# First expert of a top-2 mixture: earlier index list, transposes placed inside other products, four product banks, five output tiles

## The chip, the cores and the metric

The kernel runs on one core of one Trainium2 chip. The metric is device time in microseconds (us). Three timed runs of the kernel before gave 952.67, 953.08 and 953.52 us; the median is 953.08 us. A trace comes from one further, profiled execution that took 952.76 us.

## The reference, cut to what matters

Three stages follow one another: a linear attention with a decaying state (4 batches, 8 heads, 768 steps, head size 48), a dense block `h = ((x @ w1) * (x @ w2)) @ w3`, `y = h @ w_out`, and a mixture of 8 experts in which every row goes to its two best:

```python
logits = x @ w_gate
noisy = logits + np.log1p(np.exp(x @ w_noise)) * noise        # 3072 rows, 8 experts
top2 = np.argpartition(-noisy, 2, axis=1)[:, :2]
# softmax over the two, then per expert e, for the rows that chose it:
h = np.maximum(x[mask] @ w1[e], 0.0)                          # 384 -> 1024
out[mask] += top2_w[mask, k, None] * (h @ w2[e])              # 1024 -> 384
```

## The kernel before, in words

Rows come in 24 chunks of 128. Attention and dense block work in 12 groups of two chunks. A group `g` of the dense block has 12 steps (slots): the products of `mo_ab` with w1 (bank `bA`) and w2 (bank `bB`), and `mo_x`, which multiplies their product with the folded w3 @ w_out and accumulates in the two banks `bX`. `mo_x(g, 3)` of a group stands in the third slot of the next group; for the last group, number 11, it stands after the loop. `mo_out` then copies the gate columns into `LZ` and writes the rows to a table in HBM, `x2d` ("x_rows" in the trace). Every float32 product is made of three products of a high and a low part (`mm3`, L170 to L172), so each evicted tile is split: ScalarE writes the high part, VectorE the low one.

The gate works on batches of four chunks. `gate_top` is a generator of steps on VectorE, with two activations (exponential, logarithm with a table load before and after) on ScalarE and three small products on TensorE (L597 to L600, and L628 in the last batch). It ends with a slot number for each row and expert. `gate_put` (L638) writes row number and weight to these slots of the HBM table `slots`: one indirect DMA on GpSimd for each chunk and choice, eight a batch. The last batch but one (chunks 16 to 19) is put in slots of groups 10 and 11; the last batch (chunks 20 to 23) after group 11, beside the first expert's products.

An expert has up to 800 rows: a first half of four tiles of 128 rows, and a second of two tiles and one of 32. `need` loads the index list (`ti`, on the SyncE queue, once every put before it has landed) and gathers the rows (`xg`, indirect DMAs on GpSimd). For expert 0, `need(0, 0, ...)` takes rows of the first 20 chunks alone, so it waits for the last batch but one and not for the last; its second half takes what the last batch puts. `tr(e, hf)` transposes the gathered tiles on TensorE into banks `PB[4]` to `PB[6]` and splits them into `XTh`, `XTl`. `mm1(hf, ff)` makes one of eight blocks of the hidden layer, evicted as `HH` (high part L754 on ScalarE, low part L755 on VectorE); banks alternate between two for the first half and three for the second. `mm2(e, j)` multiplies a tile of 128 rows by w2 in eight steps of three products, scales it into an output tile `ye` (three buffers) on ScalarE, and adds it to the output with an indirect DMA on GpSimd (L780). `split_e` makes high and low parts of expert weights; `load_e` loads them.

VectorE runs in the order in which the code is written. The other engines' instructions are put in order at build time by a planner: of the instructions that its own clock says are ready, it takes the one written first. That order is then fixed; on the chip each engine goes through its list and waits where something isn't there. The functions touched by the change are `mm1`, `mm2`, the two loops over gate batches and groups, and the first expert's stretch of code after them.

Of the kernel before, what the change touches and what calls it, by code (L numbers as in the profile page):

```python
# [8 lines left out]
F32 = mybir.dt.float32  # L9
# [9 lines left out]
P = 128  # L19
B, H, S, D = 4, 8, 768, 48  # L20
DM, FF, E = 384, 1024, 8
# [3 lines left out]
NGRP = NCH // 2  # L25
# [6 lines left out]
TA, TB = 4, 2  # L32
# [39 lines left out]
def tile_kernel(ctx: ExitStack, tc: tile.TileContext, dt, nat, w3t, wout, w1, w2, e1, e2, cf, ci, out):  # L72
# [8 lines left out]
    def f(ap):  # L81
        return ap.bitcast(F32)
# [17 lines left out]
    PB = [psum.tile([P, 512], F32, name=f"pb{i}") for i in range(8)]  # L100
    bA, bB, bX, bY, bST, bK = PB[0], PB[1], (PB[2], PB[3]), PB[4], (PB[5], PB[6]), PB[7]
# [20 lines left out]
    def split(h, l, src, on=None):  # L122
        act.copy(out=h, in_=src)  # L123
        (on or dve).tensor_tensor(out=l, in0=src, in1=f(h), op=OP.subtract)  # L124
# [44 lines left out]
    def mm3(o, wh, wl, xh, xl, start, stop):  # L169
        pe.matmul(o, wh, xh, start=start, stop=False)  # L170
        pe.matmul(o, wh, xl, start=False, stop=False)  # L171
        pe.matmul(o, wl, xh, start=False, stop=stop)  # L172
# [238 lines left out]
    def at(slot, fn, *a):  # L411
        todo.setdefault(slot, []).append((fn, a))

    def run_todo(k):
        for fn, a in todo.pop(k, []):
            fn(*a)
# [101 lines left out]
    def low_p():  # L518

        while LOWP:  # L520
            l, p, h = LOWP.pop()
            dve.tensor_tensor(out=l, in0=p, in1=f(h), op=OP.subtract)

    def mo_x(g, fp):
        for tt in range(2):
            for fi in range(2):
                ff = 2 * fp + fi
                s = slice(256 * fi + P * tt, 256 * fi + P * tt + P)
                wh, wl = [w[:, ff % 4] for w in (W0, W1)[ff // 4]]
                mm3(bX[tt][:, :XW], PH[g, fp][:, s], PL[g, fp][:, s], wh, wl, ff == 0, ff == 7)  # L530

    def mo_out(g):
        for tt in range(2):
            t = 2 * g + tt
            dve.tensor_copy(out=LZ[:, t, :], in_=bX[tt][:, DM:XW])
            xo = work.tile([P, DM], F32, name="xo")
            act.copy(out=xo, in_=bX[tt][:, :DM])
            act.dma_start(out=x2d[DUMP + t * P:DUMP + P + t * P], in_=xo)
# [131 lines left out]
    EP = {}  # L670

    def open_a():
        EP["a"] = ctx.enter_context(tc.tile_pool(name="epa", bufs=1))
        XT["h"] = EP["a"].tile([P, 3, CAP], F32R, name="XTh")
        XT["l"] = EP["a"].tile([P, 3, CAP], F32R, name="XTl")
        XT["t"] = EP["a"].tile([P, DM], F32, name="xgt")
        pool.memset(XT["t"], 0.0)
        open_h(EP["a"], 0)
# [13 lines left out]
    def load_e(e, m, i):  # L692
        if m == 0 and e:
            rw = EP["b"].tile([P, 1536], F32, name="raww", bufs=2)
        else:
            rw = rawp.tile([P, 1538], F32, name="raw2", tag="raw64")[:, :1536]
        sp.dma_start(out=rw, in_=(e1, e2)[m][e, :, 1536 * i:1536 * i + 1536])
        RW[e, m, i] = rw
# [23 lines left out]
    def rows_of(j):  # L722
        return TPT if j < NT - 1 else TPL

    def ti(e, j):
        hf, jj = divmod(j, TA)
        return TI[e, hf][:rows_of(j), jj]
# [6 lines left out]
    def tr(e, hf):  # L734
        n = NAB[hf]
        for db in range(3):
            bank = PB[4 + db]
            for j in range(TA) if hf == 0 else range(TA, NT):
                o = TPT * (j - hf * TA)
                pe.transpose(bank[:, o:o + P], XG[e, j][:, P * db:P * db + P], ident)  # L740
            s = slice(hf * NAB[0], hf * NAB[0] + n)
            split(XT["h"][:, db, s], XT["l"][:, db, s], bank[:, :n])

    MB, MC, AD = (bA, bB, bK), [1], [-1]

    def mm1(hf, ff):
        n = NAB[hf]
        s0 = hf * NAB[0]
        bank = MB[ff % (2 + hf)][:, :n]
        for kb in range(3):  # L750
            w = slice(kb * FF + ff * P, kb * FF + ff * P + P)
            mm3(bank, WAh[:, w], WAl[:, w], XT["h"][:, kb, s0:s0 + n], XT["l"][:, kb, s0:s0 + n], kb == 0, kb == 2)
        n = (TA, TB)[hf] * TPT
        act.activation(out=Hh[hf][:, ff], in_=bank[:, :n], func=AF.Relu)  # L754
        dve.scalar_tensor_tensor(Hl[hf][:, ff], bank[:, :n], 0.0, f(Hh[hf][:, ff]), op0=OP.max, op1=OP.subtract)  # L755
        if hf == 1:
            dve.tensor_scalar(HM[hf][:, ff], bank[:, n:], 0.0, None, op0=OP.max)

    def mm2(e, j):
        hf, jj = divmod(j, TA)  # L760
        n, s = rows_of(j), slice(TPT * jj, TPT * jj + rows_of(j))
        MC[0] ^= 1
        bank = bX[MC[0]][:, :DM]
        y = EP["a"].tile([P, DM], F32, name="ye", bufs=3)
        wt = ti(e, j)[:, 1:2].bitcast(F32)
        if j < NT - 1:
            for ff in range(8):
                w = slice(ff * DM, ff * DM + DM)
                mm3(bank[:n], Hh[hf][:, ff, s], Hl[hf][:, ff, s], WBh[:, w], WBl[:, w], ff == 0, ff == 7)
            act.activation(out=y[:n], in_=bank[:n], func=AF.Copy, scale=wt)  # L770
        else:

            for ff in range(8):
                g = ff % 4
                pe.matmul(bank[n * g:n * g + n], HM[hf][:, ff], RW[e, 1, ff // 4][:, g * DM:g * DM + DM],  # L775
                          start=ff < 4, stop=ff > 3, tile_position=(0, n * g))
            act.activation(out=y[:n], in_=bank[:n], func=AF.Copy, scale=wt)
            for g in range(1, 4):
                dve.scalar_tensor_tensor(y[:n], bank[n * g:n * g + n], wt, y[:n], op0=OP.mult, op1=OP.add)
        ins = pool.indirect_dma_start(out=out, out_offset=bass.IndirectOffsetOnAxis(ap=ti(e, j)[:, 0:1], axis=0),  # L780
                                      in_=y[:n], in_offset=None, compute_op=OP.add).ins

        if j == 0 or AD[0] != e:
            AD[:] = [e]
        for p in AD[1:]:
            tc.declare_no_dep(ins, p, reason="an expert's rows differ")
        AD.append(ins)

    def need(e, hf, r, rows=NROW):
        load_idx(e, hf, r)  # L790
        for j in range(TA) if hf == 0 else range(TA, NT):
            gather(e, j, rows)
# [31 lines left out]
    def gate_at(o, t0, per, put):  # L824
        gen = gate_top(t0, GB)
        for i in range(10):
            at(o + i // per, next, gen, None)
        for i in range(2 * GB):
            at(o - o % SPG + put[i], gate_put, t0, i // 2, i % 2)


    for t0 in range(0, NCH - GB, GB):
        late = t0 == NCH - 2 * GB
        gate_at(SPG * ((t0 + GB) // 2) + 3, t0, 1 + late,
                (11, 11, 13, 13, 13, 14, 14, 14) if late else (13, 14, 17, 17, 19, 20, 23, 23))
    at(SPG + 2, fill_table)
    for i in range(5):
        at(2 * SPG + 6 * i, fill_out, i)
# [1 line left out]
    for g in range(NGRP):  # L840
        sub = [(mo_ab, g, 0, 0), (mo_ab, g, 0, 1), None, (mo_ab, g, 1, 0), (mo_ab, g, 1, 1), (mo_x, g, 0),
               (mo_ab, g, 2, 0), (mo_ab, g, 2, 1), (mo_x, g, 1), (mo_ab, g, 3, 0), (mo_ab, g, 3, 1), (mo_x, g, 2)]
        if g == NGRP - 1:
            attx.close()
            open_a()
            load_e(0, 0, 0)
            load_e(0, 0, 1)
        for i in range(12):
            if sub[i]:
                fn, *a = sub[i]  # L850
                fn(*a)
            elif g:
                mo_x(g - 1, 3)
                mo_out(g - 1)
            if i % 3 != 1:
                low_p()
            run_todo(SPG * g + i)
            if g == NGRP - 1:
                if i in (0, 3, 6, 9):
                    split_e(0, 0, i // 3, dve)  # L860
                    if i == 9:
                        load_e(0, 1, 0)
                        load_e(0, 1, 1)
                if i == 3:
                    need(0, 0, 0, NROW - GB * P)
    low_p()
    tr(0, 0)
    mo_x(NGRP - 1, 3)
    mo_out(NGRP - 1)
    assert not todo, todo  # L870
    t0 = NCH - GB
    gen = gate_top(t0, GB)
    for ff in range(8):
        for _ in range(2 if ff != 3 else 0):
            next(gen, None)
        mm1(0, ff)
        if ff >= 4:
            split_e(0, 1, ff - 4, dve)
    for i in range(GB):
# [5 lines left out]
    for jj in range(TA, NT):  # L885
        gather(0, jj)
    for j in range(TA):
        mm2(0, j)
        if j == 0:
            load_e(1, 0, 0)  # L890
            load_e(1, 0, 1)
            need(1, 0, 0)
    tr(0, 1)
    need(1, 1, 0)
    for ff in range(8):
        mm1(1, ff)
# [28 lines left out]
    if RMAX > 1:  # L925

        n = nc.values_load(rounds[0:1, E:E + 1], min_val=1, max_val=RMAX)
# [102 lines left out]
```

## Time and profile before

| | |
|---|---|
| timed runs, median (lowest to highest) | 953.08 us (952.67 to 953.52) |
| the profiled execution | 952.76 us, span of its trace 950.8 us |
| TensorE busy | 913.9 us, 96% of the span |
| VectorE, ScalarE, GpSimd busy | 48%, 44%, 37% |
| mean granted TensorE clock | 0.991 of full speed |

The span begins with the first instruction and ends with the last; 1.96 us lie around it. The dense block's last group ends at about 488 us, the first expert runs from there to about 552 us, and seven experts of about 55.5 us each follow. A wait names the engine and instruction that ended it.

### The profile page before, as it was taken

The numbers are of one execution on the slowest core, as the hardware profiler recorded it, in microseconds if no ns is written. First come the engines' busy times: TensorE is split into PE (matmuls) and PEld (weight loads), VectorE is DVE, ScalarE is ACT, GpSimd is POOL, SyncE is SP. The second block draws the span as 40 slices with busy tenths as digits, with TensorE's granted clock in tenths as the row PEclk, the third lists the DMA queues.
The fourth block names the chain that finished last, engine by engine and source line by source line (L and its number), as shares of the span: only waits on it lengthen the run. The fifth ranks groups of instructions, "written<-read, shape, count | busy, mean of one in ns | idle before, by whom it ended". The sixth has DMA issues, their size and how long they took to land.

```text
span 950.8 us, 17795 instructions
## 1 busy us (share of the span) xinstructions
PE 913.9 (96%) x7219; PEld 845.7 (89%) x7219; DVE 453.5 (48%) x1110; ACT 422.1 (44%) x879; POOL 347.1 (37%) x282
## 2 busy tenths in 40 slices
PE   7898999999999999999989899999999999999994
PEld 6777899999999999999979889989898998989894
DVE  5789765756756748646343263231313223131320
ACT  6767545446355445544341243433324343332420
POOL 2123100232122131140315545654557565455412
PEclk9999999999999999999999899999999999999998
DMA  9945786455242332410240464326163532614112
GB/s 359 372 148 180 192 138 205 146 155 171 79 124 79 90 112 79 132 37 18 52 150 20 86 203 149 63 66 160 39 168 62 158 62 65 161 39 103 17 20 36
DMA packets 49179, 111.64 MB, mean 117 GB/s; under 512 B 17600, under 2 KB 32192, under 8 KB 49088
## 3 DMA queue, kind: packets, MB, share of 16 engines
q1 hardware_dynamic: 33472, 85.98, 28.9%
q0 software_dynamic: 12160, 19.72, 11.5%
q10 hardware_dynamic: 3456, 4.72, 1.4%
q8 instruction: 58, 0.95, 0.5%
q14 instruction: 33, 0.27, 0.1%
HBM read 88.12 MB, written 22.27 MB: 116 GB/s over the span
## 4 chain that ended last, share of the span: by engine, by line
PE 83%; issue 4%; DVE 4%; DMA 3%; ACT 2%; POOL 2%; SPq 0%; POOLq 0%; ACTq 0%; DVEq 0%
PE pb L170 24%; PE pb L171 23%; PE pb L172 23%; PE pb L302 4%; PE pb L242 2%; PE pb L740 2%; PE pb L775 1%; PE pb L263 1%; DVE cvz L154 1%; POOL slots L643 1%; DMA slots<-g_sc,g_si 1%; DMA raw<-w 1%; PE pb L252 1%; ACT top L145 1%; DMA out<-ye,ti 1%
## 5 line engine op out<-in xcount | busy, mean ns | idle before, releaser
L170 PE MATMUL pb<-XTh,WAh 128*128 128x512 f32 (+1 forms) x384 | 134.6, 352 | 3.6 <-ACT XTh L123 3.5
L171 PE MATMUL pb<-XTl,WAh 128*128 128x512 f32 (+1 forms) x384 | 132.8, 346 | 0.0
L172 PE MATMUL pb<-XTh,WAl 128*128 128x512 f32 (+1 forms) x384 | 131.9, 346 | 0.0
L170 PE MATMUL pb<-WBh,HH 128*128 128x384 f32 x384 | 130.9, 341 | 0.7 <-ACT HH L754 0.7
L171 PE MATMUL pb<-WBl,HH 128*128 128x384 f32 x384 | 129.5, 338 | 0.0
L172 PE MATMUL pb<-WBh,HH 128*128 128x384 f32 x384 | 129.4, 337 | 0.0
L755 DVE SCALAR_TENSOR_TENSOR HH<-pb,HH 128x256 fp32r<-128x256 f32 (+1 forms) x128 | 71.4, 558 | 118.9 <-ACT HH L754 118.9
L780 POOL DMA_INDIRECT out<-ye,ti x56 | 86.8, 1550 | 112.2 <-ACT ye L770 99.0
L754 ACT ACTIVATE HH<-pb 128x256 fp32r<-128x256 f32 (+1 forms) x128 | 62.7, 491 | 130.1 <-PE pb L172 129.0
L643 POOL DMA_INDIRECT slots<-g_sc,g_si x48 | 51.5, 1073 | 119.4 <-DVE g_si L642 78.6
L770 ACT ACTIVATE ye<-pb,ti 128x384 f32<-128x384 f32 x48 | 27.9, 581 | 150.2 <-PE pb L172 102.7
L124 DVE TENSOR_TENSOR XTl<-pb,XTh 128x512 fp32r<-128x512 f32 (+1 forms) x48 | 25.3, 570 | 139.3 <-ACT XTh L123 139.2
L222 POOL TENSOR_TENSOR rku<-natc 128x384 f32<-128x384 f32 x24 | 26.9, 1119 | 174.9 <-DMA natc<-nat 103.3
L170 PE MATMUL pb<-xh,WBh 128*128 128x256 f32 x288 | 83.7, 291 | 2.9 <-DVE pp L512 2.4
L170 PEld LDWEIGHTS pb<-XTh,WAh 128*128 128x128 f32 x384 | 73.1, 191 | 14.0 <-ACT XTh L123 3.8
L170 PE MATMUL pb<-xh,WAh 128*128 128x256 f32 x288 | 82.8, 288 | 1.3 <-ACT xh L308 0.7
L172 PE MATMUL pb<-xh,WBl 128*128 128x256 f32 x288 | 81.6, 283 | 1.0 <-DVE WBl L161 1.0
L171 PE MATMUL pb<-xl,WBh 128*128 128x256 f32 x288 | 82.3, 286 | 0.0
L172 PE MATMUL pb<-xh,WAl 128*128 128x256 f32 x288 | 81.5, 283 | 0.8 <-DVE WAl L161 0.7
L171 PE MATMUL pb<-xl,WAh 128*128 128x256 f32 x288 | 81.2, 282 | 0.1
L171 PEld LDWEIGHTS pb<-XTl,WAh 128*128 128x128 f32 x384 | 73.3, 191 | 7.9
L172 PEld LDWEIGHTS pb<-XTh,WAl 128*128 128x128 f32 x384 | 72.8, 191 | 8.3
(173 smaller groups left out, 2209.0 us busy)
## 6 DMA issues: line engine op xcount, KB each, us to landing
dtc<-dt SPq DMA_DIRECT2D x24, 772.0 KB, 5.3
natc<-nat SPq DMA_DIRECT2D x24, 640.0 KB, 4.9
raw<-e SPq DMA_DIRECT2D x18, 768.0 KB, 6.3
raww<-e SPq DMA_DIRECT2D x14, 768.0 KB, 4.4
rawf<-w3t SPq DMA_DIRECT2D x16, 512.0 KB, 7.4
raw<-w SPq DMA_DIRECT2D x8, 768.0 KB, 4.4
x_rows<-xo ACTq DMA_DIRECT2D x24, 192.0 KB, 2.0
out<-zeros SPq DMA_DIRECT2D x4, 1152.0 KB, 8.1
```

The lines of the kernel that those rows point to most:

```text
L124: (on or dve).tensor_tensor(out=l, in0=src, in1=f(h), op=OP.subtract)
L170: pe.matmul(o, wh, xh, start=start, stop=False)
L171: pe.matmul(o, wh, xl, start=False, stop=False)
L172: pe.matmul(o, wl, xh, start=False, stop=stop)
L222: pool.tensor_tensor(out=t, in0=NA[j][:, :DM], in1=NA[j][:, DM:2 * DM], op=OP.mult)
L242: pe.matmul(bST[hb][:, P * a:P * a + P], KT[j][q, a].rearrange("p s i -> p (s i)"), RT[j][q, a].rearrange("p s i -> p (s i)"), start=True, ...
L302: pe.matmul(o, lt, rh, start=st, stop=en, tile_position=tp)
L643: ins = pool.indirect_dma_start(out=table, out_offset=bass.IndirectOffsetOnAxis(ap=si[:, i, k:k + 1], axis=0), in_=SC[:, i, k, :], in_offs ...
L754: act.activation(out=Hh[hf][:, ff], in_=bank[:, :n], func=AF.Relu)
L755: dve.scalar_tensor_tensor(Hl[hf][:, ff], bank[:, :n], 0.0, f(Hh[hf][:, ff]), op0=OP.max, op1=OP.subtract)
L770: act.activation(out=y[:n], in_=bank[:n], func=AF.Copy, scale=wt)
L780: ins = pool.indirect_dma_start(out=out, out_offset=bass.IndirectOffsetOnAxis(ap=ti(e, j)[:, 0:1], axis=0), in_=y[:n], in_offset=None, com ...
```

## The change

The puts of the last batch but one move from slots 11, 13 and 14 (group 10's last, and the second and third of group 11) to slots 9, 10 and 11 of group 10. `need(0, 0, ...)` moves from the fourth slot of group 11 to the second. `tr(0, 0)` moves from behind group 11 to the front of its last slot, so that two `mo_x` stand behind it and not one. The last batch's gate steps are spread otherwise over the eight `mm1(0, ff)`: before 2, 2, 2, 0, 2, 2, ... and now 5, 1, 0, 2, 1, ... These eight `mm1` go over four banks (`bA`, `bB`, `PB[4]`, `PB[5]`) in place of two. `tr(0, 1)` moves from behind `mm2(0, 3)` into its middle, before the fifth of eight steps. `ye` gets five buffers.

```diff
-    def mm1(hf, ff):
+    def mm1(hf, ff, banks=None):
         n = NAB[hf]
         s0 = hf * NAB[0]
-        bank = MB[ff % (2 + hf)][:, :n]
+        banks = banks or MB[:2 + hf]
+        bank = banks[ff % len(banks)][:, :n]
...
-    def mm2(e, j):
+    def mm2(e, j, mid=None):
...
-        y = EP["a"].tile([P, DM], F32, name="ye", bufs=3)
+        y = EP["a"].tile([P, DM], F32, name="ye", bufs=5)
...
             for ff in range(8):
+                if mid and ff == 4:
+                    mid()
...
-                (11, 11, 13, 13, 13, 14, 14, 14) if late else (13, 14, 17, 17, 19, 20, 23, 23))
+                (9, 9, 9, 10, 10, 10, 11, 11) if late else (13, 14, 17, 17, 19, 20, 23, 23))
...
         for i in range(12):
+            if g == NGRP - 1 and i == 11:
+                tr(0, 0)
...
-                if i == 3:
+                if i == 1:
                     need(0, 0, 0, NROW - GB * P)
     low_p()
-    tr(0, 0)
     mo_x(NGRP - 1, 3)
     mo_out(NGRP - 1)
...
     for ff in range(8):
-        for _ in range(2 if ff != 3 else 0):
+        for _ in range((5, 1, 0, 2, 1)[ff] if ff < 5 else 1):
             next(gen, None)
-        mm1(0, ff)
+        mm1(0, ff, (bA, bB, PB[4], PB[5]))
...
     for j in range(TA):
-        mm2(0, j)
+        mm2(0, j, (lambda: tr(0, 1)) if j == TA - 1 else None)
...
-    tr(0, 1)
     need(1, 1, 0)
```

## Rows read from the trace of the kernel before

**Rows 1.** The page, busy time of each engine: us, share, instructions.
```profile
PE 913.9 (96%) x7219; PEld 845.7 (89%) x7219; DVE 453.5 (48%) x1110; ACT 422.1 (44%) x879; POOL 347.1 (37%) x282
```

**Rows 2.** Waits of TensorE, 478 to 530 us: total us, times, longest.
```profile
PE pb L170 <- ACT XTh L123: 3.5, 1, 3.5
PE pb L740 <- DMA xg<-x_rows,ti: 2.2, 1, 2.2
PE pb L170 <- ACT HH L754: 0.7, 1, 0.7
```

**Rows 3.** TensorE by stretch: from:to, length, busy (instructions), granted clock, DMA share, GB/s.
```profile
477.88:480.06 2.18, 2.18 (x14) 1.00 0.80 207
480.06:487.84 7.78, 5.61 (x26) 0.78 0.32 133
487.84:523.30 35.46, 34.61 (x173) 1.00 0.23 69
...
527.99:540.17 12.18, 12.18 (x72) 0.76 0.62 107
540.17:544.34 4.17, 4.17 (x27) 1.00 0.00 0
544.34:545.74 1.40, 1.40 (x14) 1.00 0.00 0
551.43:552.34 0.91, 0.91 (x11) 1.00 1.04 376
552.34:569.26 16.92, 16.92 (x76) 1.00 0.63 211
569.26:578.85 9.59, 9.59 (x72) 1.00 0.01 2
```

**Rows 4.** Timeline of GpSimd: start, us, instruction, idle before it and what ended it.
```profile
452.03 0.42 POOL L677 MEMSET xgt<- 128x384 f32 x1 [25.74 <-PE pb L302]
...
467.02 1.01 POOL L643 DMA_INDIRECT slots<-g_sc,g_si  x1 [0.30 <-issue]
475.66 0.97 POOL L731 DMA_INDIRECT xg<-x_rows,ti  x1 [7.63 <-DMA ti<-slots]
...
501.76 1.01 POOL L643 DMA_INDIRECT slots<-g_sc,g_si  x1 [20.73 <-DVE g_si L623]
...
520.07 0.87 POOL L731 DMA_INDIRECT xgt<-x_rows,ti  x1 [0.30 <-issue]
```

**Rows 5.** Chain of waits, 455 to 532 us: a put from issue to landing.
```profile
467.02 5.96 DMA slots<-g_sc,g_si
...
511.39 2.74 DMA slots<-g_sc,g_si
```

**Rows 6.** Timeline of VectorE around the two gate batches and the puts.
```profile
446.46 0.22 DVE L620 TENSOR_REDUCE g_sf<-g_M 128x8 f32<-128x64 f32 x1
...
488.04 0.17 DVE L535 COPY LZ<-pb 128x16 f32<-128x16 f32 x1 [0.92 <-PE pb L172]
...
492.84 0.69 DVE L755 SCALAR_TENSOR_TENSOR HH<-pb,HH 128x512 fp32r<-128x512 f32 x1 [1.33 <-ACT HH L754]
...
496.37 0.76 DVE L584 TENSOR_TENSOR g_cm<-g_cm,g_mb 128x8 bf16<-128x8 bf16 x4
...
499.29 0.16 DVE L601 TENSOR_SCALAR g_s<-g_d 128x4 f32<-128x4 f32 x1
...
501.31 0.17 DVE L623 CAST g_si<-g_sf 128x8 int32<-128x8 f32 x1
...
505.29 0.95 DVE L710 TENSOR_TENSOR WBl<-raw,WBh 128x768 fp32r<-128x768 f32 x1
```

**Rows 7.** ScalarE ahead of the second half's splits.
```profile
527.07 0.58 ACT L770 ACTIVATE ye<-pb,ti 128x384 f32<-128x384 f32 x1 [7.19 <-DMA out<-ye,ti]
```

**Rows 8.** SyncE's queue: a weight load's issue, and waits of such loads, 440 to 545 us.
```profile
477.65 0.33 SPq L697 DMA_DIRECT2D raw<-e  x1
...
SPq L697 <- DVE WAl L710: 50.1, 2, 46.1
```

## The prediction, made before the changed kernel was run

> **What bounds the kernel now.** I read the page first: TensorE is busy 913.9 us of the 950.8 us span, the next engine 48% [rows 1]. So a change pays only where TensorE idles or runs at its lower clock, and the next view is TensorE's waits in the stretch that the change touches. There are three, 6.4 us in all [rows 2]: 2.2 us for the gathered rows in the first expert's first transposes, 0.7 us for the eviction of a bank in `mm1(0, ff)`, 3.5 us for the split of the second half's transposes. The third view, TensorE by stretch, gives each its whole price, as the granted clock shows what followed: 0.78 over the first stall and the work behind it, 0.76 over `mm1(1, ff)` behind the third, 1.00 around the second [rows 3]. [...]
>
> What each stretch would take undisturbed is read from like work:
>
> - First hole, 480.06 to 487.84: 7.78 us for twelve transposes and a `mo_x`. Undisturbed 1.40 + 2.18 = 3.58. Excess 4.20.
> - First half's products, 487.84 to 523.30: 35.46 us for eight `mm1` and four `mm2`. The next expert's eight took 16.92, a `mm2` takes 4.17, so 16.92 + 16.68 = 33.60, and about 0.05 for four tiny gate products. Excess 1.81.
> - Second hole, from 523.30 to 540.17: 16.87 us for nine transposes (0.91) and eight `mm1(1, ff)` (9.59 in the next expert). Undisturbed 10.50. Excess 6.37.
>
> All from [rows 3]; the sum, 12.38 us, is the most that the change can take away. Behind 540 us work follows without a wait of this kind and moves with it.
>
> **The change part by part, first list and first transposes.** The gate batch has its slot numbers at 446.68 us [rows 6] and GpSimd is idle for 25.74 us up to 452.03 [rows 4], so the first three puts can go out from about 447.5, while now the last starts at 467.02. Three casts then stand behind the attention's last copy at about 453; five puts at 1.27 each (0.97 busy and 0.30 of issue, [rows 4]) and the memset of 0.42 that may fall between them end by about 460. The last put starts near 458.5, 8.5 us sooner. It lands after 2.7 us or, loaded as now, 6.0 [rows 5]: 461.2 to 464.5. From landing now (472.98) to the products' restart (482.50 = 480.06 + 0.27 + 2.17) it takes 9.5 us, so the rows are there between 470.7 and 474.0. The transposes are wanted at 477.88, 2.18 us sooner than now because they stand before one more `mo_x`: 3.9 to 7.2 us to spare. The six casts and eight puts are no more than before; the SyncE queue has the list's load two slots sooner, ahead of two weight loads that wait for buffers anyway.
>
> The splits of `XTh`, `XTl` then lie beside two `mo_x` (4.36 us) in place of one. One thing is late in turn: VectorE makes three low parts of 128x512 (0.69 each for that shape, [rows 6]) before the low part that the second `mo_x` reads in its third product. Transposes done at 479.28, the last low part at about 481.1, the needed one at 481.8; wanted at 481.82. Between 0 and 0.8 us (if ScalarE takes its own product's cast first); I take 0.2. Gain 4.20 - 0.20 = **4.0 us**. `mm1(0, 0)` starts at 483.64 + 0.2.
>
> **Four banks and gate steps.** The wait of 0.7 us and what hung on it (two `mm2` steps put in its place) go, since the third block no longer needs the first's bank. The gate steps hold up the first block's low part on VectorE, but with four banks that is wanted only by the fifth block, 8.4 us after the start. The steps up to the counts end now at 497.13 [rows 6]. Shifted by 4.20, without the block that stands between them (wait 1.33 and 0.61 of its 0.69) and the next block's 0.6, they end at 490.4; three low parts of 0.6 follow, 492.2; the last steps (499.29 to 501.48, 2.19 us) end at 494.4. That is 7.1 us sooner than now. If the little exponential on ScalarE falls ahead of the second block's eviction, the low parts wait and it is 6.2; I take 6.6. The first low part is done at 491.0, wanted at 492.0: no wait.
>
> Two waits are new. The batch's count product now stands before the fourth `mm1`, which TensorE reaches at about 490.0, with the counts there at 490.4; and the batch's totals product stands in the fifth, from 492.1, and needs the slot numbers' readers, at about 493.7. All further `mm1` are queued behind both, and only TensorE waits. The planner can put them some products later, as now. Bounds 0 and 0.4, 0 and 1.6; together I take 0.8. VectorE's weight splits behind the gate end near 503.5, just as the third quarter of w2 is wanted, for nothing. Gain 1.81 - 0.80 = **1.0 us**.
>
> **Five output tiles, transposes in `mm2(0, 3)`.** Now ScalarE stands 7.19 us before the fourth `ye`, for an output add that has to land [rows 7], and the splits are queued behind it; that is the 3.5 us wait. With five buffers the fourth tile waits for nothing, and since the transposes stand before the last twelve products (2.09 us), even the splits (about 1.5 us after the transposes) are covered. What is late next is the gather. The last batch's chain is rigid from first put (501.76) to last gather (520.07) [rows 4], whose rows were there at 523.30 without a wait and, by the shortest landing of such a gather (2.3 us), not before 522.4. Shifted by 6.6 they are there between 515.8 and 516.7. TensorE wants them at 483.84 + 33.65 + 0.8 - 2.09 = 516.2. A tie: 0 to 0.5 us by these values, up to 1.6 if the gate is only 6.2 sooner and TensorE waits nowhere before. I take 0.5; a wait of 0.7 left the clock at 1.00 [rows 2, 3]. Gain 6.37 - 0.50 = **5.9 us**.
>
> [...] The eight puts take 9.63 us from the first start to the last [rows 4, 5]; seven steps at 1.01 + 0.30 make 9.2, so the VectorE work beside them, with four splits of w2 (0.95 each, [rows 6]) whose inputs both lie in SBUF, costs about 0.5 us. [...] The same splits lie beside the puts after the change.
>
> **Sum.** 4.0 + 1.0 + 5.9 = 10.9 us off the profiled execution's 952.76 (span 950.8 and 1.96 around it): 941.9. The timed runs' median is 0.32 above that execution, so I forecast 942.2 us.
>
> **Rivals.**
>
> 1. *The second half's gather is later than the tie.* The transposes stand at the head of TensorE's list with products behind them that could run. If the rows are 2 to 3 us late, TensorE waits so long and, as after the 2.2 us wait, runs on at half clock; there the excess beyond the wait was 4.20 - 2.17 = 2.0. Cost 4.0 to 5.0 in place of 0.5: gain 6.4 to 7.4, 945.7 to 946.7. For it: the chain is long, and the order is the planner's. Against it: the chain's start was worked out from measured steps. 20%.
> [...]
> 3. *The list isn't sooner.* If the last put's landing at 472.98 hangs on the transfers beside it and not on its issue, the rows come at 482.50 as now, but are wanted 2.18 us earlier: first hole 6.4 instead of none, gain 4.7, 948.4. The loaded 5.96 us against 2.74 speaks for it, the 8.5 us against it. 5%.
> 4. *Slower: the list's load is queued behind the second weight load.* These loads wait for VectorE's splits, 50.1 us for two, and the second goes out at 477.65 [rows 8]. Were the list's load behind it, the first gather would follow at about 480.3 (now 475.66) and the products restart 6.84 later, at 487.2; TensorE would idle 9.3 us from 477.88, and with 2.0 for the clock `mm1` starts 7.1 us later than now. That eats the 6.9 of the other two parts: 953.3, and by up to 3.2 us more (the loaded landing) with the weight's 768 KB in front of list and rows: 956.5. It decides from a list load after 477 us. Against it: the list's load is written before both. 6%.
>
> **How the numbers follow.** Forecast 62%, its own range 940.3 to 944.5 (nothing left of the excess, to the bounds of the new waits). Rivals 20, 3, 5 and 6%; 4% for what I don't see. The range that leaves no more than 2 in 10 out reaches over rival 1: 940.0 to 947.5. The measurement can tell about 0.2% (1.9 us) from no change: faster 0.89 (forecast, rivals 1 to 3, less 0.01), same 0.06, slower 0.05 (rival 4 and the rest, split).
>
> **What would show it.** Right: no TensorE wait on the gathered rows before 488 us; granted clock 1.00 from 477 to 545; the last put of the earlier batch near 458.5; slot numbers of the last batch near 494.9; no wait of `ye` on the output add; the next expert's first `mm1` near 541.5 in place of 552.3. Wrong: a wait on the rows of over 1 us in `mm2(0, 3)` with half clock behind it, TensorE standing before the gate's small products for over 1 us, or the list's load behind weights.

## The result, and the profile after

The changed kernel takes 943.59 us (median of five, 941.17 to 945.34), the kernel before 952.94 us beside it (five, 951.01 to 953.52). The ratio is 0.9908 [0.9889, 0.9926]. The forecast was 942.2 us, its range 940.0 to 947.5. The profiled execution took 944.56 us, its span is 942.7 us.

The page's first part: every engine's busy time is as before to 0.9 us [rows 1]. For TensorE two things cancel in it, as will be seen: less time at the lower clock behind waits, more slow products at the program's start.

```profile
PE 913.7 (97%) x7219; PEld 846.6 (90%) x7219; DVE 453.4 (48%) x1110; ACT 422.5 (45%) x879; POOL 347.7 (37%) x282
```

TensorE waits for nothing from 440 to 545 us in this trace; the three waits of [rows 2] are gone. Stretch by stretch, as in [rows 3] (from:to, length, busy time of PE, PEld, DVE, ACT and POOL, granted clock, DMA share, GB/s): the first transposes with two `mo_x`; the first half's products up to the second transposes; these with the twelve products behind them; `mm1(1, ff)`; the second half's `mm2` with the next transposes; the next expert's first eight `mm1`.

```profile
481.54:487.36 5.82, 5.82 (x38) 5.62 (x37) 3.44 (x6) 3.92 (x7) 0.00 (x0) 1.00 0.43 135
487.36:519.32 31.96, 31.92 (x162) 28.27 (x162) 15.84 (x66) 10.19 (x18) 12.38 (x13) 1.00 0.25 77
519.32:522.41 3.09, 3.09 (x22) 3.09 (x21) 1.19 (x3) 1.06 (x3) 2.48 (x3) 1.00 0.47 132
522.41:531.91 9.50, 9.50 (x73) 9.50 (x73) 3.66 (x14) 3.28 (x8) 7.67 (x7) 1.00 0.76 128
531.91:544.08 12.17, 12.17 (x88) 10.91 (x86) 5.98 (x10) 5.10 (x10) 7.46 (x6) 1.00 0.61 140
544.08:561.00 16.92, 16.92 (x76) 13.71 (x75) 9.68 (x14) 7.91 (x14) 7.20 (x6) 1.00 0.65 210
```

The clock is 1.00 in each. In the kernel before it is 0.50 from 483.00 to 485.50, behind the first wait, and 1.00 from 486.00 to 488.00; 0.50 again from 528.00 to 533.00, behind the third, and 1.00 from 534.00 to 540.00. These two values are the half and the full clock of this text; 0.78 and 0.76 [rows 3] are means over stretches that hold both. From the last `mo_ab` to `mm1(0, 0)` it takes 5.82 us (before, 477.87 to 487.84, 9.97), from there to the end of `mm1(1, ff)` 44.55 (before 52.33): 4.15 and 7.78, together 11.9 us less. The rest of the span is as long as before (410.79, before 410.63). But the span is only 8.1 us shorter, because the last `mo_ab` ends 3.67 us later, at 481.54. That comes from the very start of the program; the section on the prediction returns to it.

GpSimd, to be held against [rows 4]: first, fourth and last put of the earlier batch, its first gather, first and last put of the last batch, the first gather behind it.

```profile
451.27 1.00 POOL L643 DMA_INDIRECT slots<-g_sc,g_si  x1 [21.32 <-DVE g_si L642]
...
456.94 1.28 POOL L643 DMA_INDIRECT slots<-g_sc,g_si  x1 [0.82 <-DVE g_si L642]
...
462.90 0.97 POOL L643 DMA_INDIRECT slots<-g_sc,g_si  x1 [0.30 <-issue]
469.45 0.97 POOL L731 DMA_INDIRECT xg<-x_rows,ti  x1 [5.58 <-DMA ti<-slots]
...
498.54 1.01 POOL L643 DMA_INDIRECT slots<-g_sc,g_si  x1 [24.35 <-DVE g_si L623]
...
508.06 0.97 POOL L643 DMA_INDIRECT slots<-g_sc,g_si  x1 [0.30 <-issue]
514.07 0.98 POOL L731 DMA_INDIRECT xg<-x_rows,ti  x1 [5.04 <-DMA ti<-slots]
```

The earlier batch's first gather goes out at 469.45 in place of 475.66, in a program that is 3.67 us late: 9.9 us sooner. SyncE has the list's load (L719) ahead of the weight loads, not behind them [rows 8]:

```profile
466.46 0.33 SPq L719 DMA_DIRECT2D ti<-slots  x1
468.30 13.35 SPq L697 DMA_DIRECT2D raw<-e  x2
```

VectorE's gate [rows 6]: the last copy into `LZ` (the first product starts at 487.36), the counts, the first block's low part (now L756), the slot numbers.

```profile
487.56 0.17 DVE L535 COPY LZ<-pb 128x16 f32<-128x16 f32 x1 [0.55 <-PE pb L172]
...
493.51 0.75 DVE L584 TENSOR_TENSOR g_cm<-g_cm,g_mb 128x8 bf16<-128x8 bf16 x4
494.19 0.68 DVE L756 SCALAR_TENSOR_TENSOR HH<-pb,HH 128x512 fp32r<-128x512 f32 x1
...
498.09 0.17 DVE L623 CAST g_si<-g_sf 128x8 int32<-128x8 f32 x1
```

ScalarE around the second half's splits [rows 7]: no wait on the output add. The three casts follow one another; remember this for the last experiments.

```profile
519.84 1.06 ACT L123 CAST XTh<-pb 128x288 fp32r<-128x288 f32 x3 [1.86 <-PE pb L740]
522.61 0.58 ACT L773 ACTIVATE ye<-pb,ti 128x384 f32<-128x384 f32 x1 [1.71 <-PE pb L172]
523.80 0.39 ACT L755 ACTIVATE HH<-pb 128x256 fp32r<-128x256 f32 x1 [0.61 <-PE pb L172]
```

### The profile page after: what moved, and what is told of

It is laid out like the page before. It is cut to its first block, busy times and chain, and to the rows that moved or that the text cites. A ratio compares the mean times of both kernels' runs of the same rounds, so it can differ in the third digit from the quotient of the medians.

```text
span 942.7 us, 17789 instructions
## 1 busy us (share of the span) xinstructions
PE 913.7 (97%) x7219; PEld 846.6 (90%) x7219; DVE 453.4 (48%) x1110; ACT 422.5 (45%) x879; POOL 347.7 (37%) x282
## 4 chain that ended last, share of the span: by engine, by line
PE 90%; DVE 4%; ACT 2%; issue 2%; POOL 0%; DMA 0%; POOLq 0%; SPq 0%; DVEq 0%; ACTq 0%
PE pb L170 27%; PE pb L171 26%; PE pb L172 26%; PE pb L302 4%; PE pb L242 2%; PE pb L740 2%; PE pb L778 1%; PE pb L263 1%; DVE cvz L154 1%; PE pb L252 1%; DVE w3l L161 1%; ACT top L145 1%; PE pb L373 1%; ACT am L235 0%; DVE WBl L161 0%
## 5 line engine op out<-in xcount | busy, mean ns | idle before, releaser
L756 DVE SCALAR_TENSOR_TENSOR HH<-pb,HH 128x256 fp32r<-128x256 f32 (+1 forms) x128 | 71.3, 557 | 116.1 <-ACT HH L755 116.1
```

## The experiments

Each kernel's profile is cut in four, so that the start's share stands apart: "start" to the end of the last `mo_ab`; "hole 1" from there to `mm1(0, 0)`; "half" from there to the end of `mm1(1, ff)`; "rest". They add up to the span of that one execution. Medians are of the timed runs (their number), ratios against the kernel before run beside them. `e9` to `e12` ran on another chip than the eight ahead of them.

| kernel | median us (n) | ratio | start | hole 1 | half | rest |
|---|---|---|---|---|---|---|
| before | 952.94 (5) | | 477.87 | 9.97 | 52.33 | 410.63 |
| after | 943.59 (5) | 0.9908 [0.9889, 0.9926] | 481.54 | 5.82 | 44.55 | 410.79 |
| e1_list_back | 951.31 (10) | 0.9977 [0.9962, 0.9992] | 481.44 | 13.61 | 44.54 | 410.71 |
| e2_tr1_back | 942.14 (4) | 0.9891 [0.9870, 0.9912] | 478.47 | 5.70 | 44.50 | 410.73 |
| e3_two_banks | 944.91 (6) | 0.9923 [0.9896, 0.9949] | 478.31 | 5.83 | 47.69 | 410.87 |
| e4_gate_back | 945.92 (4) | 0.9923 [0.9905, 0.9941] | 482.43 | 5.82 | 46.09 | 410.76 |
| e5_three_tiles | 943.54 (4) | 0.9895 [0.9864, 0.9926] | 477.77 | 5.81 | 44.71 | 410.61 |
| e6_tr2_back | 944.04 (4) | 0.9894 [0.9859, 0.9929] | 480.29 | 5.82 | 44.91 | 410.78 |
| e7_list_alone | 948.76 (7) | 0.9952 [0.9932, 0.9973] | 478.32 | 5.82 | 50.91 | 410.85 |
| e8_tiles_alone | 947.73 (7) | 0.9941 [0.9922, 0.9960] | 478.36 | 9.86 | 46.34 | 410.64 |
| e9_warm_after | 945.08 (6) | 0.9922 [0.9902, 0.9941] | 478.67 | 5.81 | 47.38 | 410.84 |
| e10_warm_before | 951.56 (12) | 0.9990 [0.9978, 1.0002] | 476.83 | 9.75 | 51.05 | 411.07 |
| e11_after_again | 948.42 (6) | 0.9952 [0.9937, 0.9967] | 481.95 | 5.82 | 48.92 | 410.71 |
| e12_before_again | 952.70 (12) | 0.9996 [0.9982, 1.0009] | 478.15 | 9.90 | 50.83 | 410.72 |

The start alone runs from 476.83 to 482.43, more than most parts are worth. So parts are judged by "hole 1" and "half", and by the medians only where these differ widely.

**List back, transposes still early.** The changed kernel with the puts and the list's load in their old slots.

```diff
-                (9, 9, 9, 10, 10, 10, 11, 11) if late else (13, 14, 17, 17, 19, 20, 23, 23))
+                (11, 11, 13, 13, 13, 14, 14, 14) if late else (13, 14, 17, 17, 19, 20, 23, 23))
...
-                if i == 1:
+                if i == 3:
                     need(0, 0, 0, NROW - GB * P)
```

> The changed kernel with its slot writes and its index list put back to the old places; the transposes stay early, before the last two mo_x. Theory (the three holes are separate, and the list's earlier issue is what makes the rows be there in time): the last put starts near 470 us in that trace's time (or 8 us after the changed kernel's 462.90), the rows come 4 to 5 us after TensorE wants them, and it runs on at half clock: from the first transpose to the first mm1 11 to 13 us (changed kernel 5.82, before 9.96 with one mo_x more ahead of the transposes). Total 948.5 to 951. Rival (the list hangs on the transfers beside it and not on its issue): the rows come as in the changed kernel, 5.8 to 6.5 us, total within 1 us of the changed kernel's 943.6.

TensorE's waits and the stretch of the first hole (same columns as above; the clock is the 0.75):

```profile
PE pb L740 <- DMA xg<-x_rows,ti: 3.9, 1, 3.9
PE pb L740 <- PE pb L172: 0.7, 1, 0.7
```

```profile
481.44:495.05 13.61, 8.92 (x39) 8.01 (x37) 3.50 (x6) 3.97 (x7) 2.47 (x3) 0.75 0.31 105
```

Hole 1 grows by 7.79 us to 13.61, above the 11 to 13 expected (and the median, 951.31, lies just above the 951), while the rest of the first expert stays (44.54). Of it 4.69 us are idle and 3.10 us slower products (busy 8.92 for 5.82). It is also 3.64 us longer than in the kernel before, 2.5 of them idle time (4.69 us against 2.17): transposes that are asked for sooner than their rows come make the hole larger. The early list is what counts.

**First transposes back.** The changed kernel with `tr(0, 0)` behind group 11.

```diff
-            if g == NGRP - 1 and i == 11:
-                tr(0, 0)
...
     low_p()
+    tr(0, 0)
     mo_x(NGRP - 1, 3)
```

> The changed kernel with the first transposes back behind group 11, so that one mo_x and not two stands between them and mm1; list early. Theory (the list alone closes the first hole; one mo_x of 2.18 us nearly covers the splits): no wait on the gathered rows, mo_x to mm1 5.8 to 6.4 us, total 943 to 945. Rival (the splits need the second mo_x as cover): TensorE waits 0.8 to 1.5 us for the split before mm1, 6.6 to 7.5 us, total 944.5 to 946.

No wait, hole 1 is 5.70, a little under what I expected and not longer than with the transposes early. With rows that are there in time, one `mo_x` covers the splits as well as two. In this kernel the early place of the transposes is worth nothing (0.1 us the other way).

**Two banks.** The changed kernel with `mm1(0, ff)` on two banks.

```diff
-        mm1(0, ff, (bA, bB, PB[4], PB[5]))
+        mm1(0, ff)
```

> The changed kernel with two product banks for the first half in place of four; five gate steps still ahead of the first block's low part. Theory (the four banks are what lets the gate go first): the third block waits for the first's low part, done 7.5 us after mm1's start, so TensorE waits 3 to 4 us there and runs at half clock for some time behind it; mm1 and mm2 of the first half take 38 to 41 us without the nine transposes (changed kernel 34.1, before 35.5), total 946.5 to 950. Rival (the planner fills the wait with mm2 products): 35 to 36 us, total 944 to 945.5.

```profile
PE pb L170 <- ACT HH L755: 0.7, 1, 0.7
PE pb L170 <- DVE HH L756: 0.6, 1, 0.6
PE pb L598 <- DVE g_cm L584: 0.5, 1, 0.5
PE pb L597 <- DVE g_mb L581: 0.5, 1, 0.5
```

The half takes 3.14 us more, between theory and rival. The bunched gate steps hold up the low parts; with two banks that reaches TensorE in four short waits, 2.3 us in all, and the planner filled part of it with `mm2` products. The clock stayed at 1.00 behind all four. So the five gate steps at once rest on the four banks.

**Gate steps back.** The changed kernel with the old spread.

```diff
-        for _ in range((5, 1, 0, 2, 1)[ff] if ff < 5 else 1):
+        for _ in range(2 if ff != 3 else 0):
```

> The changed kernel with the last gate batch spread 2, 2, 2, 0, 2, 2 as before. Theory (the second half's gather has under 0.5 us to spare in the changed kernel, so the slot numbers' time is the gather's): slot numbers 2 us later against mm1's start (10.7 us in the changed kernel), TensorE waits 1 to 2 us for the rows in the middle of the last mm2 of the first half, with or without half clock behind it; total 945 to 947.5. Rival (there is more to spare than I think): no wait, total within 0.7 us of 943.6.

```profile
PE pb L740 <- DMA xg<-x_rows,ti: 1.0, 1, 1.0
PE pb L740 <- DMA xgt<-x_rows,ti: 0.3, 1, 0.3
```

The half is 1.54 us longer, 1.3 of it these waits; the products of 128x288 behind them start every 0.13 us, as the changed kernel's do at clock 1.00. The last batch's first gather goes out 28.63 us behind `mm1(0, 0)` (516.88 against 488.25), in the changed kernel 26.71 (514.07 against 487.36), and TensorE is at the transposes 0.18 sooner (31.78 behind it, not 31.96). A chain 2.1 us later makes a wait of 1.3, so the changed kernel has some 0.8 us to spare. That is the tie of the prediction, and it fell on the good side.

**Three tiles.** The changed kernel with `bufs=3` for `ye`.

```diff
-        y = EP["a"].tile([P, DM], F32, name="ye", bufs=5)
+        y = EP["a"].tile([P, DM], F32, name="ye", bufs=3)
```

> The changed kernel with three output tiles in place of five; all else, the order on every engine too, is the same. Theory (with the transposes inside mm2 the splits stand before the fourth tile on ScalarE, so the tiles' wait can no longer hold them, only the evictions behind it): the fourth tile waits for the first output add (about 526 us in the changed kernel's time), mm1 of the second half runs on through its three banks and then waits 0.5 to 2 us; total 944 to 946. Rival (five tiles are what closes the second hole): a wait of 3.5 us or more and half clock, total 948.5 to 951.

```profile
516.07 1.06 ACT L123 CAST XTh<-pb 128x288 fp32r<-128x288 f32 x3 [1.86 <-PE pb L740]
520.78 0.58 ACT L773 ACTIVATE ye<-pb,ti 128x384 f32<-128x384 f32 x1 [3.66 <-DMA out<-ye,ti]
```

The fourth `ye` does wait for the output add, 3.66 us of idle ScalarE, but the splits now stand before it, and the three banks of `mm1(1, ff)` cover the late evictions: TensorE waits for nothing, and the half is 0.16 us longer. My expectation of a visible wait fell.

**Second transposes back.** The changed kernel with `tr(0, 1)` behind `mm2(0, 3)` and five tiles.

```diff
-        mm2(0, j, (lambda: tr(0, 1)) if j == TA - 1 else None)
+        mm2(0, j)
...
+    tr(0, 1)
     need(1, 1, 0)
```

> The changed kernel with the second half's transposes back behind the fourth mm2; five tiles. Theory (what the place inside mm2 covers is the splits, about 1 us): TensorE waits 0.7 to 1.5 us between the transposes and the first full block of mm1(1), clock stays at 1.00; total 944 to 945.5. Rival (the place of the transposes is the main thing): a wait of 3 us and half clock, total 948 or more.

The half is 0.36 us longer, less than expected. The planner starts `mm1(1, 0)` with the three products that need only the casts. In the changed kernel either edit alone closes the second hole.

**List alone, tiles alone.** The kernel before with one part each: the early puts, list and first transposes; or five tiles.

```diff
+                (9, 9, 9, 10, 10, 10, 11, 11) if late else (13, 14, 17, 17, 19, 20, 23, 23))
...
+            if g == NGRP - 1 and i == 11:
+                tr(0, 0)
...
+                if i == 1:
                     need(0, 0, 0, NROW - GB * P)
```

> The kernel before with only the first list's part of the change: slot writes and list sooner, first transposes before the last two mo_x. Theory (holes separate): first hole gone, first transpose to mm1 5.8 to 6.2 us (before 9.96 from the same mo_x on), the second hole as before (16.5 to 17 us from the second transposes to the end of mm1(1)), total 948.5 to 949.5. Rival (the second list's chain takes the gain back): second hole longer by 2 to 4 us, total 951 to 953.

```diff
-        y = EP["a"].tile([P, DM], F32, name="ye", bufs=3)
+        y = EP["a"].tile([P, DM], F32, name="ye", bufs=5)
```

> The kernel before with only five output tiles. Theory (the third wait, 3.5 us on the split, is ScalarE's wait for the output add): the wait shrinks to 0.7 to 1.5 us, the clock stays at 1.00 behind it; the second hole 11.2 to 13 us in place of 16.87; total 948 to 950. Rival (the rows or the splits bind anyway): second hole 15.5 us or more, total 951.5 to 953.

The waits of the first, then of the second:

```profile
PE pb L170 <- ACT XTh L123: 3.0, 1, 3.0
PE pb L170 <- ACT HH L754: 0.7, 1, 0.7
```

```profile
PE pb L740 <- DMA xg<-x_rows,ti: 2.1, 1, 2.1
PE pb L170 <- ACT HH L754: 0.7, 1, 0.7
```

The list alone takes 4.15 us from hole 1 and leaves the other two waits; the tiles alone take 5.99 us from the half and leave the other two (4.49 against the half of `e12`, the other profile of the kernel before). In the medians 4.3 and 5.3 us less than the kernel before beside them (953.01). So the holes are independent, and of the two parts tried alone one word, `bufs=5`, is the larger. Both second holes came out shorter than I expected. With the list alone it takes 15.4 us (from the second transposes at 519.64 to 535.05; expected 16.5 to 17), as in `e12` (15.3). With the tiles alone it takes 10.8 us without any wait for the splits (expected 11.2 to 13, with a wait of 0.7 to 1.5), and the median of 947.73 is just below the 948 to 950. The four banks and the gate steps were not tried alone on the kernel before, nor put back together: their share is read from the stages.

**The kernels again, with and without early products.** Before and after once more, and both with twelve products of 128x512 bf16 on a constant, the first that TensorE does (their result goes nowhere). The question was whether the start is what blurs the medians; `e11` and `e12` are the two kernels without an edit.

```diff
+    warm = const.tile([P, 512], BF16, name="warm")
+    dve.memset(warm, 1.0)
+    for _ in range(12):
+        pe.matmul(PB[7], warm[:, :P], warm, start=True, stop=True)
```

> The changed kernel with twelve products of a constant tile (128x512, bf16) on TensorE ahead of its first real work, into a bank that is overwritten later. In the profiles so far the last group's products end between 477.8 and 482.4 us in kernels whose code up to there is the same, and the later ones ran their first products longer at the lower clock. Theory (the start's clock sets that time, by chance, and not the change): with TensorE busy from the start the first real products run at the full clock by 8 us; the last group's products end between 474.5 and 478; single runs lie within 2.5 us of each other; median 937.5 to 941. Rival (the loads set it): same spread, same end as without, median 942 to 945.

> The kernel before with the same twelve products. Theory: the same time before the first expert as in the changed kernel with them (within 0.7 us), median 948.5 to 952, so that the two differ by 10.5 to 13 us, nearer to the 11.8 that the stages add up to than the timed 9.4. Rival: no difference to the kernel before, 952 to 954.

> The changed kernel once more, nothing else, for a second profile of its start and a second set of times. Theory: from the last group's products on 461.0 to 461.4 us as in the first profile; the time before them anywhere between 477.8 and 482.4; median 941 to 944. Rival (the change makes the start later): before them 481 or later again.

> The kernel before once more, nothing else. Theory: from the last group's products on 472 to 475 us (two half-clock stretches whose lengths vary), the time before them anywhere between 477.8 and 482.4. Rival (the change makes the start later): before them 478.5 or sooner, as in the first profile.

The kernel before came out as it had: from the last `mo_ab` on 471.45 us (472.93 in its first profile), just under the 472 that I expected. Both forms of the changed one missed what I expected: 948.42 us without the early products and 945.08 us with them, and in the profile of `e11` TensorE has one wait that the changed kernel's first profile has not; `e9` has the same, of the same length.

```profile
PE pb L170 <- DVE HM L758: 2.2, 1, 2.2
```

```profile
PE pb L174 <- DVE HM L762: 2.2, 1, 2.2
```

The first is `e11`'s, the second `e9`'s. ScalarE in `e11`, to be held against the three rows above of the same instructions:

```profile
520.25 0.40 ACT L123 CAST XTh<-pb 128x288 fp32r<-128x288 f32 x1 [1.86 <-PE pb L740]
521.62 0.40 ACT L123 CAST XTh<-pb 128x288 fp32r<-128x288 f32 x1 [0.97 <-PE pb L740]
523.03 0.40 ACT L123 CAST XTh<-pb 128x288 fp32r<-128x288 f32 x1 [1.01 <-PE pb L172]
525.95 0.58 ACT L773 ACTIVATE ye<-pb,ti 128x384 f32<-128x384 f32 x1 [2.52 <-PE pb L172]
528.12 0.38 ACT L755 ACTIVATE HH<-pb 128x256 fp32r<-128x256 f32 x1 [1.59 <-PE pb L172]
```

The nine transposes run from 519.73 to 520.87, so the second and third cast soon have their input, yet each comes 1.0 us after the cast before it; the products that the profile names were done. `ye` starts 3.0 us after its last product (522.98), in the first profile 0.03 us after (522.61, product done at 522.58). The first evictions of `mm1(1, ff)` come late in turn, TensorE waits 2.2 us for a bank, and the stretch to the end of `mm1(1, ff)` takes 13.87 us at clock 0.88 in place of 9.50 at 1.00 (in `e9`, behind the same wait, the products start every 0.13 us as ahead of it, and the half is 2.8 us longer, not 4.4):

```profile
522.82:536.69 13.87, 11.55 (x73) 11.10 (x73) 4.02 (x15) 3.56 (x9) 9.54 (x8) 0.88 0.67 117
```

That is the 4.4 us of "half". A further 0.7 us lies in group 11, behind a 0.3 us gap before a product of the attention with nothing waited for. The order of instructions on ScalarE, VectorE, GpSimd and SyncE is the same as in the first profile; on TensorE only products of the attention at that gap start in another order. What makes ScalarE late stays open: the other chip, or something of that build that these views don't show. `e12` and `e10`, same chip, have no such gap, and none of the eight earlier kernels has. All six timed runs of `e11` lie between 946.98 and 949.30, so it isn't a matter of one execution.

The early products bring the first full pace forward. The trace's record of the granted clock, which begins with 1.00, begins at 4.8 us in `e10` and 5.7 in `e9`, against 12.0 in `e12` and 17.3 in `e11`; the starts are 476.83 and 478.67 in place of 478.15 and 481.95 (`e9` and `e11` both hold the 0.7 us of group 11), one profile each, and that of `e9` is above the 474.5 to 478 that I expected. They don't make the timed runs agree better, which was the question: those of `e9` lie 5.3 us apart (2.3 in `e11`), where I had expected 2.5, and those of `e10` 4.2 (4.0 in `e12`). The median of `e9` is 3.3 us below that of `e11`; their spans differ by 4.7, 3.3 in the start and 1.5 in the half, where the pace differs behind the same wait. For the kernel before it is 1.1 us, with a ratio that doesn't exclude none. With early products the two kernels' medians are 6.5 us apart, not the 10.5 to 13 that I expected.

## Why the prediction was right, and where not

The forecast was 1.4 us under the median and inside its own range. By its steps:

- **First list** (gain 4.0): 4.15. The last put started at 462.90, less the late start 459.2, forecast 458.5. The 0.7 us are a put that waited 0.82 us for a cast on VectorE and took 1.28. Slot writes, list and gathers came in the forecast order, and the list's load stood before the weights: rivals 3 and 4 fell. Wrong was to count the transposes' early place as part of the gain. `e2` shows it is worth nothing, `e1` that it costs 3.6 us more than before without the early list.
- **Four banks and gate steps** (1.0): the first half with `mm1(0, ff)` and `mm2`, without the 0.9 us of transposes, takes 34.1 us against 35.46: 1.3. That is 0.5 above the undisturbed 33.65, where I had put 0.8 for two new waits; TensorE has neither, since the planner set the small products between others (counts at 493.51, their product at 494.12). The 0.5 lies in busy time (31.92 of 31.96 us up to the transposes), and what lengthens it is not shown. No experiment gives the part's worth by itself; `e3` shows that the early gate steps need the four banks. The slot numbers came at 498.09, less the late start 494.4; with their 0.17 us 494.6, forecast near 494.9.
- **Five tiles and transposes in `mm2(0, 3)`** (5.9): transposes and `mm1(1, ff)` take 0.9 + 9.50 against 16.87: 6.5. The half microsecond for the gather's tie wasn't needed, by a margin of some 0.8 us (`e4`). Rival 1 stood as near as I made it. The split of the gain between the two edits was not asked; `e5` and `e6` show that each alone would do.
- **Puts beside VectorE's splits**: the eight puts take 9.52 us from first start to last, before 9.63, both times about half a microsecond above seven steps of 1.27 to 1.32. Four splits of w2 lie beside them. In the changed kernel three of these (from 501.17, 502.65 and 504.12) lie over puts of 0.97 us each, the fourth (505.96 to 506.91) over the put of 1.50 us that holds the half microsecond; in the kernel before two lie over puts of 0.97 to 1.01 us, two over those of 1.44 and 1.16. That the splits lengthen a put was my estimate and is not shown. Nor does any run show what the 3% among the chances stood for: the puts are no longer than before.
- **What would show it**: no wait, clock 1.00, no wait of `ye`. The next expert's first `mm1` stands at 544.08, forecast 541.5. Less the late start it is at 540.4.

So the sum was 10.9 us and the stages gave 11.9; of the 1.5 us set aside for new waits in the three terms 0.5 was spent, and not on waits. The profiled execution is nevertheless at 944.56 and not 941, for one thing that I did not price: the start. The rows (from:to, length, TensorE busy, instructions, clock, DMA), before and after:

```profile
0.00:477.87 477.87, 459.64 (x4591) 1.00 0.47 143
```

```profile
0.00:481.54 481.54, 464.66 (x4591) 1.00 0.47 143
```

The same 4591 products are 5.0 us longer busy. In the timeline the difference begins with the first fold products: in the kernel before they run at full pace from 12.09 us, in the changed one from 18.06.

```profile
11.18 0.48 PE L172 MATMUL pb<-WBh,w3l 128*128 128x400 f32 x1
...
12.36 0.34 PE L171 MATMUL pb<-WBl,w3h 128*128 128x400 f32 x1
12.54 0.34 PE L172 MATMUL pb<-WBh,w3l 128*128 128x400 f32 x1
```

```profile
12.96 0.54 PE L171 MATMUL pb<-WBl,w3h 128*128 128x400 f32 x1
13.29 0.54 PE L172 MATMUL pb<-WBh,w3l 128*128 128x400 f32 x1
...
18.33 0.35 PE L171 MATMUL pb<-WBl,w3h 128*128 128x400 f32 x1
18.52 0.34 PE L172 MATMUL pb<-WBh,w3l 128*128 128x400 f32 x1
```

One such product every 0.33 us against one every 0.18 makes 1.8, not far from the 2 between the clock's values of 1.00 and 0.50 in these traces; that the clock was at 0.50 there is my estimate from the pace. The column of the granted clock reads 1.00 for both stretches, but the trace's record of the clock begins only at 11.5 us (before) and 17.7 us (changed), with 1.00, just where the pace changes; for the time ahead the column has no record. Later the changed kernel's profile loses a little more: between 80 and 90 us its granted clock is 0.83 (0.50 from 83.00 to 85.50), the kernel before's 1.00.

The other profiles without early products show the same tie. In seven the record begins at 11.5 to 12.5 us and the start takes 477.8 to 478.5; in five it begins at 16.4 to 19.2 and the start takes 480.3 to 482.4. So the start's length goes with the moment at which the record begins. What sets that moment is not settled. The order of instructions alone doesn't: `e5`, with the same order on every engine as the changed kernel, is among the early ones (11.6 us, start 477.77), with the same median (943.54). Its profiled execution, at 940.78, is the lowest of its four runs; the changed kernel's, at 944.56, the second highest of five. But the four profiles of the kernel before and its variants are all early, and of the eight of the changed kernel and its variants five are late, so a part of the change in it is not excluded.

That the median, 9.4 us less than before, came so near the forecast is therefore in part luck: the holes gave 11.9 us where I had counted 10.9, and the timed runs show less than the stages do.

And the size did not hold in the last runs. There the changed kernel won 4.3 us (948.42 against 952.70 beside it): by its profile, ScalarE's late casts took 4.4 back in the half, and the gap in group 11 0.7; 4.3 + 4.4 + 0.7 is the 9.4 of the first comparison, though this sets one profile's stages beside medians. I had named no such rival: an engine that, as far as these views show, waits for nothing and is late all the same.

## What to carry to other kernels

Price a wait with the stretch behind it, and as a range: with waits of 6.4 us, 11.9 us went away, but the same wait of 2.2 us cost 2.8 us in `e9` and 4.4 in `e11`. When two edits aim at one wait, try each alone: here, in the changed kernel, one buffer count closes what a rewritten loop closes, and moving a consumer earlier without its producer costs more than it can bring. Where runs of one kernel differ by as much as the parts are worth, cut the profile into stages and compare these, and time the result on a second chip before its size is believed.

## What the hardware showed that I had not expected

- The start, the same work in the same order up to group 10, took 477.77 to 482.43 us in twelve profiles, by when the clock's record begins (11.5 to 19.2 us); in the two kernels' first profiles the products of 128x400 start every 0.33 us ahead of that moment and every 0.18 behind it. What TensorE had done before doesn't tell the two apart: it was busy without a pause from 7.5 us on in the kernel before, whose record begins at 11.5, and from 7.3 in the changed one, where it begins at 17.7. With twelve constant products ahead of them it was 1.3 and 3.3 us shorter than in the same kernel without, one profile each.
- A wait of the same length is not always followed by the same loss. Behind the wait of 2.2 us the stretch's clock fell to 0.88 in `e11`; in `e9` the products went on at one every 0.13 us. `mm1(1, ff)` behind the kernel before's wait of 3.5 us took 12.18 us at clock 0.76 [rows 3]; in `e12`, behind one of 3.3 us, 10.89 at 0.87:

```profile
527.99:538.88 10.89, 10.89 (x72) 10.89 (x73) 4.59 (x16) 3.23 (x9) 7.64 (x7) 0.87 0.67 122
```

- ScalarE started casts about 1.0 us and an output tile 3 us after their inputs, in two profiles on one chip, with ScalarE's order there unchanged. Its cost is shown, 2.2 us of wait and 2.8 (`e9`) or 4.4 us (`e11`) in all; its cause is not.
